# Softmax powers in 16-bit groups of four tiles on VectorE, with TensorE adding two terms

## The chip, the cores and the metric

The kernel runs on one core of one Trainium2 chip. The metric is device time in microseconds (us) for one execution. Before the change three runs took 917.80, 919.02 and 920.45 us; the median is 919.02 us. Engines are named as the profile names them: PE is TensorE (matmul), PEld its weight loads, DVE is VectorE, ACT is ScalarE, POOL is GpSimd, SP issues DMAs.

## The reference

Two attention blocks read the same input `x` (2048 x 512) and are mixed by a gate.

```python
S, D, H, Dh = 2048, 512, 32, 16
g = sigmoid((x * gate_w).sum(-1))                 # one number for each row
# A: linear attention; the feature maps are softmaxes over 16 features, of p and of -p
pq, pk = q @ w_phi, k @ w_phi                     # per head
phi = concat(softmax(p), softmax(-p))             # 32 features, for q and for k
a = (phi_q @ (phi_k.T @ v)) / (phi_q @ sum(phi_k) + 1e-6) @ wo_A
# B: full softmax attention, 32 heads of 16
b = softmax(q @ k.T * 0.25) @ v @ wo_B
out = g * a + (1 - g) * b
```

## The kernel before

Block B carries most of the work. Its scores are computed transposed: a *tile* is 128 keys by 512 queries of one head. The work is cut into 32 *blocks* (4 query chunks x 8 groups of four heads), each of 4 heads x 16 key tiles, so 2048 tiles in all. Four heads lie in four row strips of TensorE, and up to four score products (L624, `qk_mm`, 32 rows each) run side by side in it. The scores are scaled so that the number is already an exponent: multiplied by log2(e) and 2^23.

Tiles are handed out in *slots*. In slot j `add_qk` writes up to three tiles into three PSUM banks of `psS` (banks 0 to 2 for even j, 3 to 5 for odd j), `add_exp` (L687) turns them into powers with one ScalarE instruction over 1536 (or 1024) columns, and `add_pv` (L700) multiplies the powers with the values in four column strips, summing in the bank `psO`. An extra column of ones in `vaug` sums the powers, so that `add_norm` can divide at the block's end. The score product of slot j+2 may start once the exponential of slot j is done.

152 of the 2048 tiles, the *D tiles*, do not go to ScalarE. In a slot with a D tile the exponential covers two tiles and VectorE takes the third bank: `add_d` stores the scaled score as an int32 with the bits of a float (D1, L666), takes the mantissa (D2, L677), and multiplies with a cubic in the mantissa (D4 to D6, L679 to L681). 122 late D tiles go in pairs of 1024 columns in fp32, 30 early ones alone in 512 columns. One value product per D tile is added to a later slot's `add_pv`. The cubic's leading factor is in the exponential's bias.

Block A is cut into small steps that are put between the slots. `phi` makes a feature map for 128 rows: product (L482), VectorE copy to `Pf` (L871), maximum and minimum over 16 features (L875, L877), POOL subtracts twice (L880, L883), ScalarE exponentiates 1024 columns (L886), VectorE sums and inverts (L890, L892), POOL multiplies (L894). It runs 32 times. `q_rest` and `kv_half` do the linear attention, `out_tile`, `out_pre` and `out_post` the output products. All these use one PSUM bank, `psM` (`MISC = [bM]`). The gate is computed in `gate` and multiplied in at the normalisations (`rg` at L765 for B, `nc` at L947 for A).

What sets the order: `Plan.layout` is a list scheduler written in the kernel. It has a guess of each step's duration and a priority, and from these it writes one fixed instruction list per engine, with semaphore waits. On the chip each engine takes its list strictly in that order. Where the plan sees TensorE with too little to do it adds dummy products of 512 columns: in front of a slot's scores (L642) and into `psM` (L1025); 577 in all.

## Time and profile before

| | us |
|---|---|
| median of three runs | 919.02 |
| profiled execution, from first to last instruction | 917.8 |
| ACT busy | 889.2 (97%) |
| PE busy, dummy products among it | 800.0 (87%) |
| DVE busy | 730.3 (80%) |
| POOL busy | 151.2 (16%) |

The span of the profiled execution, 917.8 us, equals the time of the lowest run, so nothing measurable lies around it; it stands 1.2 us under the median. Busy time of an engine counts overlapping instructions once. ACT and DVE instructions overlap a little at their ends, so that the rows by shape add up to more than the engine's busy time.

### The profile page before, as it was taken

Reading aid. Unit: us, or ns where it says so; the run is one execution under the profiler, and the core shown is the slowest. Engines: PE = TensorE matmul, PEld = TensorE weight load, DVE = VectorE, ACT = ScalarE, POOL = GpSimd, SP = SyncE. Lnnn points to the kernel's source line nnn. Section 1 sums busy time; section 2 is a strip of 40 time slices with the busy share of each in tenths; the row PEclk is TensorE's granted clock in tenths of the full one; section 3 lists DMA queues with packets and bytes.
Section 4 is the critical chain, followed back from the end, with each engine's and each line's share of the span. In section 5 each row is a group of like instructions: output and inputs, shape, how many; then the busy total and the mean of one; then the engine's idle time right before and its main releaser. Section 6 shows DMA issues by size and latency. Waiting matters only on the chain.

```text
span 917.8 us, 13911 instructions
## 1 busy us (share of the span) xinstructions
PE 800.0 (87%) x5801; PEld 251.3 (27%) x5903; DVE 730.3 (80%) x1114; ACT 889.2 (97%) x720; POOL 151.2 (16%) x131
## 2 busy tenths in 40 slices
PE   8889889889888889888878978888989998898988
PEld 3232323222222322223223222222222222222222
DVE  2567787788797887978988898799878877787884
ACT  6999999999999999999989999999999999999996
POOL 5000022234155501410330150020000000000000
PEclk9999999999999999999989999999999999999999
DMA  7500000000000000000000000000000000000000
GB/s 138 139 1 1 1 1 2 1 1 1 1 1 1 1 7 6 7 1 7 1 1 1 1 1 1 1 12 7 6 1 2 18 6 1 1 1 1 1 1 23
DMA packets 18959, 9.30 MB, mean 10 GB/s; under 512 B 13265, under 2 KB 18897, under 8 KB 18897
## 3 DMA queue, kind: packets, MB, share of 16 engines
q1 hardware_dynamic: 16928, 8.00, 3.7%
q8 instruction: 46, 0.75, 0.4%
q10 hardware_dynamic: 1584, 0.39, 0.2%
q0 software_dynamic: 384, 0.02, 0.1%
q14 instruction: 17, 0.13, 0.1%
HBM read 3.69 MB, written 2.10 MB: 6 GB/s over the span
## 4 chain that ended last, share of the span: by engine, by line
ACT 72%; DVE 16%; PE 11%; issue 1%
ACT E_t L687 71%; PE psS L624 3%; PE psM L482 3%; DVE stat_t L890 2%; PE psO L700 2%; PE psS L642 1%; DVE vA_t L680 1%; DVE Pf_t L871 1%; DVE vA_t L679 1%; ACT EA_t L886 1%; DVE WB_t L681 1%; DVE vA_t L666 1%; DVE vA_t L677 1%; DVE denr_t L947 1%; DVE stat_t L892 1%
## 5 line engine op out<-in xcount | busy, mean ns | idle before, releaser
L687 ACT ACTIVATE E_t<-psS 128x1536 bf16<-128x1536 f32 (+1 forms) x683 | 861.4, 1406 | 12.4 <-PE psS L624 11.6
L624 PE MATMUL psS<-qz_t,kTB_t 32*128 32x512 bf16 x2048 | 271.0, 387 | 28.0 <-ACT E_t L687 15.3
L700 PE MATMUL psO<-E_t,vaug_t 128*32 128x512 bf16 (+1 forms) x1914 | 268.8, 392 | 0.8 <-ACT E_t L687 0.6
L642 PE MATMUL psS<-WoA_t,ident_t 128*128 128x512 bf16 x327 | 115.6, 390 | 57.0 <-ACT E_t L687 52.3
L666 DVE TENSOR_SCALAR vA_t<-psS 128x512 int32<-128x512 f32 x122 | 83.6, 685 | 56.6 <-PE psS L624 55.7
L624 PEld LDWEIGHTS psS<-qz_t,kTB_t 32*128 32x128 bf16 x2048 | 66.5, 91 | 219.0 <-ACT E_t L687 110.2
L700 PEld LDWEIGHTS psO<-E_t,vaug_t 128*32 128x32 bf16 (+1 forms) x1914 | 65.7, 92 | 154.5 <-issue 141.2
L880 POOL TENSOR_TENSOR Dd_t<-Pf_t,stat_t 128x512 bf16<-128x512 f32 x32 | 37.9, 1186 | 306.5 <-DVE stat_t L875 275.5
L679 DVE SCALAR_TENSOR_TENSOR vA_t<-vA_t 128x1024 f32<-128x1024 f32 x61 | 78.0, 1279 | 1.4
L680 DVE SCALAR_TENSOR_TENSOR vA_t<-vA_t 128x1024 f32<-128x1024 f32 x61 | 76.2, 1248 | 1.0
L681 DVE SCALAR_TENSOR_TENSOR WB_t<-vA_t 128x1024 bf16<-128x1024 f32 x61 | 73.8, 1210 | 0.3
L1025 PE MATMUL psM<-WoA_t,ident_t 128*128 128x512 bf16 x190 | 63.1, 386 | 1.2 <-issue 1.1
L642 PEld LDWEIGHTS psS<-WoA_t,ident_t 128*128 128x128 bf16 x367 | 28.6, 97 | 122.7 <-ACT E_t L687 115.4
L700 PE MATMUL psO<-WB_t,vaug_t 128*32 128x512 bf16 (+1 forms) x122 | 47.2, 392 | 0.0
L894 POOL TENSOR_TENSOR phiQ_t<-EA_t,stat_t 128x1024 bf16<-128x1024 bf16 x16 | 31.5, 1977 | 85.7 <-DVE stat_t L892 67.8
L677 DVE TENSOR_SCALAR vA_t<-vA_t 128x1024 int32<-128x1024 int32 x61 | 44.4, 729 | 1.2
L894 POOL TENSOR_TENSOR phiK_t<-EA_t,stat_t 128x1024 bf16<-128x1024 bf16 x16 | 31.8, 1988 | 64.4 <-DVE stat_t L892 47.8
L482 PE MATMUL psM<-Wp_t,xT_t 128*128 128x512 bf16 x119 | 37.9, 396 | 3.6 <-DVE vA_t L863 1.8
L890 DVE TENSOR_REDUCE stat_t<-EA_t 128x64 f32<-128x1024 bf16 x32 | 38.4, 1205 | 1.5 <-ACT EA_t L886 1.4
L883 POOL TENSOR_TENSOR Dd_t<-stat_t,Pf_t 128x512 bf16<-128x512 f32 x32 | 38.1, 1192 | 0.4 <-DVE stat_t L877 0.4
L482 PE MATMUL psM<-xT_t,WB_t 128*128 128x512 bf16 x109 | 33.2, 384 | 4.3 <-issue 1.0
L760 DVE STREAM_TRANSPOSE Tf_t<-psO 128x512 f32<-128x512 f32 x32 | 22.6, 707 | 17.2 <-PE psO L700 17.1
(109 smaller groups left out, 651.4 us busy)
## 6 DMA issues: line engine op xcount, KB each, us to landing
out_dram<-WvA_t SPq DMA_DIRECT2D x16, 128.0 KB, 1.7
WB_t<-in_B_wqkv_dram SPq DMA_DIRECT2D x3, 384.0 KB, 4.8
Dd_t<-in_A_x_dram SPq DMA_DIRECT2D x4, 128.0 KB, 3.4
WvA_t<-in_A_wqkv_dram SPq DMA_DIRECT2D x1, 512.0 KB, 5.0
WoA_t<-in_A_wo_dram SPq DMA_DIRECT2D x1, 512.0 KB, 5.0
WoB_t<-in_B_wo_dram SPq DMA_DIRECT2D x1, 512.0 KB, 5.9
WB_t<-in_B_wqkv_dram ACTq DMA_DIRECT2D x3, 128.0 KB, 3.4
xT_t<-in_A_x_dram SPq DMA_TRANSPOSE x12, 4.1
```

The lines of the kernel that those rows point to most:

```text
L482: return [lambda e, ap, i=i: e.matmul(ap, lhsT=lhs[i], rhs=rhs[i], start=(i == 0), stop=(i == len(lhs) - 1)) for i in range(len(lhs))]
L624: return e.matmul(bank, lhsT=kT_B[32 * i:32 * i + 32, hg // 2, 128 * kt:128 * (kt + 1)], rhs=qz[32 * i:32 * i + 32, (b // 8) % 2, hg, :], ...
L642: e.matmul(psS[:, 512 * base:512 * (base + 1)], lhsT=ident[:], rhs=WoA[:, 0, :], start=True, stop=True)
L666: add(0.70, -45, lambda e: e.tensor_scalar(dp.t[bt].bitcast(I32)[:, 512 * half:512 * half + 512], bank, EXPB, -2.0 ** 31, op0=ALU.add, op1 ...
L679: add(f2, -20, lambda e: e.scalar_tensor_tensor(u, m, C2, m, op0=ALU.add, op1=ALU.mult), rm, [("U",)], "D4")
L680: add(f2, -20, lambda e: e.scalar_tensor_tensor(u, u, C1, m, op0=ALU.add, op1=ALU.mult), rm + ru, [("U",)], "D5")
L681: add(f2, -20, lambda e: e.scalar_tensor_tensor(dp.e[be][:, 0:w], u, C0, t, op0=ALU.add, op1=ALU.mult), ru + rt, [("E", be)], "D6")
L687: op = P.add("act", 0.07 + 0.000833 * 512 * n, 0.0, lambda e: e.activation(Ebuf[:, j % ERING, 0:512 * n], psS[:, 512 * base:512 * (base + ...
L700: return e.matmul(psO[32 * i:32 * i + w, :], lhsT=vaug[:, kt, VW * h:VW * h + w], rhs=rhs, start=start, stop=stop, tile_position=(0, 32 * ...
L890: P.add("dve", 1.22, prio, lambda e: e.tensor_reduce(stat[:, b, 1, :], e3, AX.X, ALU.add), reads=[("EA", b)], writes=[("ss", b)], name=f"s ...
L894: P.add("pool", 2.0, prio, lambda e: e.tensor_tensor(dst.rearrange("p (g f) -> p g f", f=DH), e3, stat[:, b, 1, :].unsqueeze(2).to_broadca ...
L1025: P.idle = (bM, 0.05, lambda e: e.matmul(psM[:], lhsT=ident[:], rhs=WoA[:, 0, :], start=True, stop=True), P.writer["WoA"][0])
```

## The change

It does six things.

1. The D tiles are *groups*: one key tile for all four heads of a block, 4 x 512 columns. `NG` lists the groups per block, 78 in all, so 312 D tiles; ScalarE keeps 1736 tiles. Blocks 18 to 29 have three and four groups in turn.
2. The arithmetic is 16 bits wide. The score is scaled by 2^7, so that an int16 has the bits of a bf16 number t. Per group VectorE runs D1 four times (512 columns out of PSUM, L671), D2 (mantissa with the exponent of 0.5, L680), D3 (the power of two alone, L682) and D4 (t times D2's result, L684), the last three over 2048 columns. The cubic is gone: the two terms, D3's and D4's, each get a value product, and TensorE sums them in `psO` (`add_pvd`, eight products per group). The bias of the exponential is gone with the cubic's factor.
3. Slots have three and two tiles in turn, with banks 0 to 2 and 3 to 4. The sixth bank, `bS[5]`, joins `psM` as a second bank for everything else. A D tile's scores (`dq`) are products of their own into one of these two banks. The scheduler may let such a product ride: placed directly behind a slot's score products, in a row strip that they leave free; the terms in the same way behind `add_pv`.
4. `phi` has no shift any more: ScalarE exponentiates p and -p straight from PSUM, in two instructions of 512 columns (L877). The copy, the maximum, the minimum and both POOL subtractions go.
5. The gate is one column of small products and one exponential; 1-g multiplies the output rows in `out_tile`, `out_pre` and `out_post`, and e^(logit) multiplies block A in its normalisation. `rg` and `nc` go.
6. The first groups use the buffers of `WoA` and `WoB` and half of `oT` as working space; the two weight loads come after them. Dummy products, 577 before, are 191.

The order on TensorE in the last third of the program, where no step of block A is left. L624 and L700 are the score and value products of a slot, `E_t` holds ScalarE's powers, `WB_t` those of D tiles, L642 is a dummy, L482 an output product. Before:

```order
L624 MATMUL psS<-qz_t,kTB_t 128x512 x3
L700 MATMUL psO<-E_t,vaug_t 32x512 x2
L700 MATMUL psO<-WB_t,vaug_t 32x512
L482 MATMUL psM<-WoB_t,oT_t 128x512 x2
L624 MATMUL psS<-qz_t,kTB_t 128x512 x3
L700 MATMUL psO<-E_t,vaug_t 32x512 x3
L642 MATMUL psS<-WoA_t,ident_t 128x512 x2
```

After, at a like place (L610 and L704 are the same products; `vA_t` and `Tx_t` hold terms of D tiles):

```order
L610 MATMUL psS<-qz_t,kTB_t 128x512 x3
L704 MATMUL psO<-E_t,vaug_t 32x512 x3
L704 MATMUL psO<-vA_t,vaug_t 32x512
L610 MATMUL psS<-qz_t,kTB_t 128x512 x2
L704 MATMUL psO<-E_t,vaug_t 32x512 x2
L704 MATMUL psO<-vA_t,vaug_t 32x512 x3
L704 MATMUL psO<-Tx_t,vaug_t 32x512
L610 MATMUL psS<-qz_t,kTB_t 128x512 x4
L704 MATMUL psO<-E_t,vaug_t 32x512 x3
L704 MATMUL psO<-Tx_t,vaug_t 32x512 x2
L610 MATMUL psS<-qz_t,kTB_t 128x512 x2
L610 MATMUL psM<-qz_t,kTB_t 128x512
```

Slots of three and two tiles now alternate, terms stand directly behind the slot's value products, and a D tile's score product stands behind a slot's (the fourth of "x4", and the one into `psM`).

The order on VectorE in the same part of the program. Before, one pair of late D tiles with the first step of the next:

```order
L666 TENSOR_SCALAR vA_t<-psS 128x512
L677 TENSOR_SCALAR vA_t<-vA_t 128x1024
L679 SCALAR_TENSOR_TENSOR vA_t<-vA_t 128x1024
L680 SCALAR_TENSOR_TENSOR vA_t<-vA_t 128x1024
L666 TENSOR_SCALAR vA_t<-psS 128x512
L681 SCALAR_TENSOR_TENSOR WB_t<-vA_t 128x1024
```

After, one group with steps of its neighbours (L780 belongs to a block's normalisation):

```order
L671 TENSOR_SCALAR Tx_t<-psS 128x512
L780 TENSOR_TENSOR TB_t<-Tf_t,rd_t 128x16x16
L671 TENSOR_SCALAR Tx_t<-psM 128x512
L671 TENSOR_SCALAR Tx_t<-psS 128x512
L680 TENSOR_SCALAR WB_t<-Tx_t 128x2x1024
L682 TENSOR_SCALAR vA_t<-Tx_t 128x2048
L671 TENSOR_SCALAR Tx_t<-psM 128x512
L684 TENSOR_TENSOR Tx_t<-Tx_t,WB_t 128x2048
```

Three fp32 steps with two inputs have become one with 16-bit inputs, and the first steps of D tiles now empty `psM` and `bS[5]` (shown as psS), not a slot's bank.

The diff, cut to what the prediction speaks of:

```diff
-C3 = 0.10644611
-C2 = -6.64634687
-C1 = 12.93904106
-C0 = -16.68089397
-ESCALE = math.log(2.0) / 2.0 ** 23
-EBIAS = -math.log(C3)
-DLAG = 10
-
-D_RATE = ((14, 0.17), (196, 0.0), (226, 0.22), (420, 0.31))
-D_SWITCH = 210
+QSCALE = 0.25 * LOG2E * 2.0 ** 7
+EXPB = 127.0 * 2.0 ** 7 - 75.0
+ESCALE = math.log(2.0) / 2.0 ** 7
+
+NG = (0,) + (2,) * 7 + (1,) + (2,) * 9 + (3, 4) * 6 + (2, 1)
+G_EARLY = 8
+D_FIRST = 12
...
+                ride = None
+                if e == "pe" and last_pe is not None and busy[e] > t - 1e-6:
+                    want = {"qk": "dq", "pv": "term"}[last_pe]
+                    for item in sorted(queues[e]):
+                        o = item[2]
+                        if o.kind == want and not used_heads & set(o.heads):
+                            if o.acq is not None:
+                                bs = [b for b in o.acq.banks if b.free and b.shared]
+                                if not bs:
+                                    continue
+                                o.acq.bank = min(bs, key=lambda b: max([0.0] + [x.end for x in b.last]))
+                            ride = item
+                            break
+                    if ride is not None:
+                        queues[e].remove(ride)
+                        heapq.heapify(queues[e])
+                        pick = ride[2]
+                        pick.dur = RIDE
+                        used_heads |= set(pick.heads)
...
-    MISC = [bM]
+    MISC = [bM, bS[5]]
...
+    groups = [[dict(b=b, kt=NT - 1 - k) for k in range(NG[b])] for b in range(NB)]
...
+        act = [t for t in (next_tile() for _ in range(3 - j % 2)) if t is not None]
...
+    vfree = vAf[:, 0:8192].rearrange("p (n c) -> p n c", c=2048)
+    flat = lambda ap: ap.rearrange("p a b -> p (a b)")
+    bufs = {"x0": (Tx[:, 0, :], ()), "x1": (Tx[:, 1, :], ()), "woA": (flat(WoA[:]), ()), "woB": (flat(WoB[:]), ()),
+            "oT1": (flat(oT[:, 1, :, :]), ()), "a0": (vfree[:, 0, :], va_free), "a1": (vfree[:, 1, :], va_free),
+            "a2": (vfree[:, 2, :], va_free), "a3": (vfree[:, 3, :], va_free),
+            "w0": (W_B[:, 0:2, D:3 * D], kv_mm), "w1": (W_B[:, 2:4, D:3 * D], kv_mm)}
+    rings = {True: (("x0", "x1"), ("woB", "oT1"), "woA"), False: (("x0", "x1", "a0", "a1"), ("w0", "a2", "a3"), "w1")}
+    count = {True: 0, False: 0}
...
-            op.take = [bS[3], bS[4], bS[5]]
+            op.take = [bS[3], bS[4]]
...
+    def add_group(g):
+        b, hg, kt = g["b"], g["b"] % 8, g["kt"]
+        t, s, m = (bufs[g[k]][0] for k in "tsm")
+        ft, ops = opening(g["t"]), []
+        before = list(dq_ops)
+        dq_ops.clear()
+        for q in range(4):
+            f, mm = fill(d_prio(g), [lambda e, ap, q=q: qk_mm(e, (b, q, kt), ap)],
+                         [("kT", hg // 2, kt // 4), ("q", (b // 8) % 2, hg)], name=f"dq{b}.{kt}.{q}", dur=0.27,
+                         after=[exp_ops[D_FIRST]] + ft + P.writer.get((g["t"], q), []) +
+                         P.readers.get((g["t"], q), []) + before, cols=240)
+            dq_ops.append(mm)
+            mm.kind, mm.heads = "dq", [q]
+            ops.append(drain(f, mm, "dve", 0.70, d_prio(g), lambda e, ap, q=q: e.tensor_scalar(
+                quarter(t, q).bitcast(I16), ap, EXPB, 0.0, op0=ALU.add, op1=ALU.max),
+                writes=[(g["t"], q)], after=ft, name=f"D1.{b}.{kt}.{q}"))
+
+        def add(dur, fn, reads, writes, name, after=()):
+            ops.append(P.add("dve", dur, d_prio(g) - 5.0, fn, reads=reads, writes=writes, after=after,
+                             name=f"{name}.{b}.{kt}"))
+        tk = [(g["t"], k) for k in range(4)]
+        mi, si16, ti16 = m.bitcast(I16), s.bitcast(I16), t.bitcast(I16)
+        add(0.72, lambda e: e.tensor_scalar(shaped(mi, mi), shaped(ti16, mi), 0x007F, 0x3F00, op0=ALU.bitwise_and,
+                                            op1=ALU.bitwise_or), tk, [g["m"]], "D2", opening(g["m"]))
+        add(0.72, lambda e: e.tensor_single_scalar(shaped(si16, si16), shaped(ti16, si16), 0x7F80, ALU.bitwise_and),
+            tk, [g["s"]], "D3", opening(g["s"]))
+        add(1.24, lambda e: e.tensor_tensor(shaped(t, m), shaped(t, m), m, ALU.mult), [g["m"]], tk, "D4")
+        if g["early"]:
+            early_ops.extend(ops)
 
     def add_exp(j):
...
-            Ebuf[:, j % ERING, 0:512 * n], psS[:, 512 * base:512 * (base + n)], ACTF.Exp, bias=EBIAS, scale=ESCALE),
+            Ebuf[:, j % ERING, 0:512 * n], psS[:, 512 * base:512 * (base + n)], ACTF.Exp, scale=ESCALE),
...
+    def add_pvd(g, started):
+        b, kt = g["b"], g["kt"]
+        ops = []
+        for which in "st":
+            for i in range(4):
+                ap = quarter(bufs[g[which]][0], i)
+                op = P.add("pe", 0.26, T_PRIO, lambda e, ap=ap, i=i: pv_mm(e, (b, i, kt), ap, False, False),
+                           reads=[(g["t"], i) if which == "t" else g["s"], ("v", (b % 8) // 2, kt // 4), "v1", "v2"],
+                           after=[started], name=f"pvd{which}{i}.{b}.{kt}")
+                op.full = 0.05
+                op.kind, op.heads = "term", [i]
+                ops.append(op)
+        if g["early"]:
+            early_ops.extend(ops)
...
-        P.add("dve", 0.2, -40, lambda e: e.tensor_tensor(rd[:, bb, :], rd[:, bb, :], gT[:, 2, 16 * qc:16 * qc + 16],
-                                                         ALU.mult), reads=[("rd", bb), "omg"], writes=[("rd2", bb)],
-              name=f"rg{b}")
...
-        drain(f, mm, "dve", 0.69, 0, lambda e, ap: e.tensor_copy(fin[:, tile % 4, :], ap),
-              writes=[("fin", tile % 4)], after=va_ops, name=f"Oe{tile}")
+        drain(f, mm, "dve", 0.69, 0, lambda e, ap: e.tensor_scalar(
+            fin[:, tile % 4, :], ap, omg[:, tile:tile + 1], None, op0=ALU.mult),
...
+        drain(f, mm, "act", 0.25, -5, lambda e, ap: e.activation(egate, ap[:, 0:NT], ACTF.Exp), writes=["eg"],
+              name="ge")
+        P.add("dve", 0.1, 20, lambda e: e.tensor_single_scalar(gT[:, 1, :], egate, 1.0, ALU.add), reads=["eg"],
               writes=["g1"], name="g1")
-        P.add("dve", 0.3, 20, lambda e: e.reciprocal(gT[:, 0, :], gT[:, 3, :]), reads=["g1"], writes=["g"], name="g2")
...
-        drain(f, mm, "dve", 0.69, prio, lambda e, ap: e.tensor_copy(Pf[:, b, :], ap), writes=[("Pf", b)],
-              name=f"Pe{qk}.{st}")
-        p3 = Pf[:, b, :].rearrange("p (h f) -> p h f", f=DH)
-        mx, mn = stat[:, b, 0, 0:32], stat[:, b, 0, 32:64]
-        P.add("dve", 0.68, prio, lambda e: e.tensor_reduce(mx, p3, AX.X, ALU.max), reads=[("Pf", b)],
-              writes=[("mx", b)], name=f"mx{qk}.{st}")
-        P.add("dve", 0.68, prio, lambda e: e.tensor_reduce(mn, p3, AX.X, ALU.min), reads=[("Pf", b)],
-              writes=[("mn", b)], name=f"mn{qk}.{st}")
-        dv = Dd[:, b, :].rearrange("p (h f) -> p h f", f=32)
-        P.add("pool", 1.1, prio, lambda e: e.tensor_tensor(
-            dv[:, :, 0:DH], p3, mx.unsqueeze(2).to_broadcast([128, H, DH]), ALU.subtract),
-            reads=[("Pf", b), ("mx", b)], writes=[("D", b, 0)], name=f"d0{qk}.{st}")
-        P.add("pool", 1.1, prio, lambda e: e.tensor_tensor(
-            dv[:, :, DH:32], mn.unsqueeze(2).to_broadcast([128, H, DH]), p3, ALU.subtract),
-            reads=[("Pf", b), ("mn", b)], writes=[("D", b, 1)], name=f"d1{qk}.{st}")
-        ex = P.add("act", 1.2, -4, lambda e: e.activation(EA[:, b, :], Dd[:, b, :], ACTF.Exp),
-                   reads=[("D", b, 0), ("D", b, 1)], writes=[("EA", b)], name=f"ex{qk}.{st}")
-        ex.margin = 1.0
+        def both(e, ap):
+            for sgn in range(2):
+                ins = e.activation(EA[:, b, :].rearrange("p (g s c) -> p s g c", s=2, c=64)[:, sgn, :, :],
+                                   ap.rearrange("p (g c) -> p g c", c=64), ACTF.Exp, scale=1.0 - 2.0 * sgn)
+            return ins
+        drain(f, mm, "act", 0.98, -4, both, writes=[("EA", b)], name=f"ex{qk}.{st}")
...
-            P.add("dve", 0.2, -3, lambda e, dr=dr: e.tensor_tensor(dr, dr, g128[:, i:i + 1].to_broadcast([128, 16]),
-                                                                   ALU.mult),
-                  reads=[("dr", b, rnd), "g128"], writes=[("dr", b, rnd)], name=f"nc{i}.{rnd}")
...
+                return e.scalar_tensor_tensor(dst, num, egate[:, i:i + 1],
+                                              dr3.unsqueeze(3).to_broadcast([128, 4, 4, 16]), ALU.mult, ALU.mult)
```

290 lines of the change are left out of this document (114 added, 176 removed).

## The prediction

> **What bounds the kernel now.** I read the page's busy times and its chain of waits first, then the groups by shape, then ACT's waits, then stretches of time. From the page:
>
> ```profile
> PE 800.0 (87%) x5801; PEld 251.3 (27%) x5903; DVE 730.3 (80%) x1114; ACT 889.2 (97%) x720; POOL 151.2 (16%) x131
> ACT 72%; DVE 16%; PE 11%; issue 1%
> L687 ACT ACTIVATE E_t<-psS 128x1536 bf16<-128x1536 f32 (+1 forms) x683 | 861.4, 1406 | 12.4 <-PE psS L624 11.6
> ```
>
> ScalarE is the bound: 97% busy, and 861.4 of its 889.2 us are the exponentials of L687. They waited 12.4 us in all, nearly all of it for score products. So the change is worth what it takes off ScalarE, less what new waits put into ScalarE's queue. The groups by shape give the prices (count, then busy us and mean ns of one):
>
> ```profile
> L687 ACT ACTIVATE E_t<-psS 128x1536 bf16<-128x1536 f32 x530 | 739.6, 1500 | 10.1 <-PE psS L624 9.3
> L687 ACT ACTIVATE E_t<-psS 128x1024 bf16<-128x1024 f32 x153 | 165.2, 1080 | 2.3 <-PE psS L624 2.3
> L666 DVE TENSOR_SCALAR vA_t<-psS 128x512 int32<-128x512 f32 x122 | 83.6, 685 | 56.6 <-PE psS L624 55.7
> L679 DVE SCALAR_TENSOR_TENSOR vA_t<-vA_t 128x1024 f32<-128x1024 f32 x61 | 78.0, 1279 | 1.4
> L680 DVE SCALAR_TENSOR_TENSOR vA_t<-vA_t 128x1024 f32<-128x1024 f32 x61 | 76.2, 1248 | 1.0
> L681 DVE SCALAR_TENSOR_TENSOR WB_t<-vA_t 128x1024 bf16<-128x1024 f32 x61 | 73.8, 1210 | 0.3
> L677 DVE TENSOR_SCALAR vA_t<-vA_t 128x1024 int32<-128x1024 int32 x61 | 44.4, 729 | 1.2
> L886 ACT ACTIVATE EA_t<-Dd_t 128x1024 bf16<-128x1024 bf16 x32 | 35.8, 1120 | 0.2 <-POOL Dd_t L883 0.2
> L679 DVE SCALAR_TENSOR_TENSOR phiQT_t<-phiQT_t 128x512 f32<-128x512 f32 x30 | 21.1, 703 | 0.5
> L871 DVE COPY Pf_t<-psM 128x512 f32<-128x512 f32 x32 | 21.8, 682 | 10.8 <-PE psM L482 10.6
> L875 DVE TENSOR_REDUCE stat_t<-Pf_t 128x32 f32<-128x512 f32 x32 | 21.5, 671 | 0.5
> L947 DVE TENSOR_TENSOR denr_t<-denr_t,g_t 128x16 f32<-128x16 f32 x32 | 11.3, 354 | 0.6
> L760 DVE STREAM_TRANSPOSE Tf_t<-psO 128x512 f32<-128x512 f32 x32 | 22.6, 707 | 17.2 <-PE psO L700 17.1
> L932 DVE COPY phiQT_t<-psM 128x1024 bf16<-128x1024 bf16 x16 | 11.0, 685 | 6.0 <-PE psM L929 5.7
> ```
>
> Then stretches of time. The columns are the stretch, its length, busy us (and instructions) of PE, PEld, DVE, ACT and POOL, the granted clock, and two of DMA. The last row is clean running late in the program; the others are steps of 3.4 us around places where the clock falls to half, and one where it doesn't:
>
> ```profile
> 367.40:370.80 3.40, 1.59 (x13) 0.51 (x14) 3.40 (x7) 3.39 (x3) 0.00 (x0) 0.99 0.00 0
> 370.80:374.20 3.40, 3.40 (x17) 0.65 (x14) 3.18 (x5) 2.57 (x2) 0.72 (x1) 0.50 0.14 43
> 469.80:473.20 3.40, 1.70 (x12) 0.48 (x12) 3.40 (x6) 3.40 (x3) 1.93 (x1) 0.99 0.02 5
> 473.20:476.60 3.40, 2.63 (x14) 0.68 (x14) 2.20 (x7) 0.81 (x2) 0.00 (x0) 0.50 0.00 0
> 476.60:480.00 3.40, 3.40 (x21) 0.94 (x20) 2.13 (x4) 2.19 (x3) 0.00 (x0) 0.50 0.00 0
> 480.00:483.40 3.40, 3.40 (x25) 1.45 (x25) 2.12 (x3) 3.05 (x3) 1.26 (x1) 0.50 0.00 0
> 230.80:234.20 3.40, 1.96 (x25) 0.88 (x23) 2.65 (x4) 3.40 (x4) 0.00 (x0) 1.00 0.00 0
> 720.00:780.00 60.00, 54.37 (x366) 15.49 (x372) 46.63 (x57) 60.00 (x51) 0.00 (x0) 1.00 0.02 8
> ```
>
> In 720 to 780 us ScalarE never waits. Where it does, a step in which PE was busy for half the time only (1.59, 1.70 us) is followed by steps at clock 0.50, and there ScalarE loses time: 13.6 us from 469.8 to 483.4 held 9.45 us of it, a loss of 4.1 us for 10.2 us at half clock.
>
> **ScalarE, term by term.** The two shapes of L687 differ by one tile of 512 columns and by 1500 - 1080 = 420 ns, so a tile costs 0.420 us. The 683 instructions held 530 x 3 + 153 x 2 = 1896 tiles; 861.4 - 1896 x 0.420 = 65.1 us is left, 0.095 us for an instruction (waits inside the busy time included). After, 312 tiles instead of 152 go to VectorE, so ScalarE has 1736 in 695 instructions:
> - 160 tiles fewer: -67.2 us. 12 instructions more: +1.1 us.
> - Feature maps: 64 instructions of 512 columns for 32 of 1024. The columns are the same; 32 more instructions cost +3.0 us, and reading PSUM (1080 ns for 1024 columns, against 1120 from SBUF) gives back 1.3 us.
> - The bias goes and the gate's exponential is narrower; no row prices either apart, and I take nothing, between -1 and +1 us.
>
> ScalarE's busy time becomes 889.2 - 64.4 = 824.8 us. It was idle for 917.8 - 889.2 = 28.6 us. The start and the end make most of that:
>
> ```profile
> 11.25 9.51 ACT E_t L687 x7
> 904.58 2.70 ACT E_t L687 x2
> 911.21 0.18 DVE rd_t L765
> 912.65 1.04 PE psS L482 x4
> ```
>
> The first exponential starts at 11.25 us, with some 3 us of ScalarE work before it, and the chain after the last (end about 909.5) takes 8.3 us: 8.2 + 8.3 = 16.5 us. The change leaves the first block's loads and projections as they are and takes 0.2 us (L765) from the end: 16.3. Idle in between was 28.6 - 16.5 = 12.1 us, over half of it at half clock. Two things move it.
>
> *Short slots.* Behind a two-tile exponential the next scores have 420 ns less time. ScalarE's whole wait for them was this, beside POOL's and VectorE's on the shared bank:
>
> ```profile
> ACT E_t L687 <- PE psS L624: 11.6, 19, 2.6
> PEld psM L482 <- DVE Pf_t L871: 8.9, 15, 1.6
> ```
>
> 153 short slots become 347. If short slots carried all 11.6 us it would grow by 347/153 to 26 (+15); if they carry none, +0. Late in the program, where nearly one slot in three is short, ScalarE reads 60.00 of 60.00, which is nearer to the lower end: I take +4.
>
> *Clock.* 191 dummies remain of 577, and groups of two tiles fill less of the array. Terms that ride count nothing as time. I take half as much clock loss again, +4; the ends are below.
>
> 824.8 + 16.3 + 12.1 + 8 = **861 us** for the profiled execution; a median would stand about 1 above. Since the per-instruction 0.095 us was taken with waits in it, some of these 8 are counted twice, and I say **858**.
>
> **VectorE: does it hide?** Removed: 456 us of D tiles (83.6 + 78.0 + 76.2 + 73.8 + 44.4 for the late ones; the thirty early ones, five steps of 512 columns at about 0.67 us like L679's 703 ns, 100), 64.8 of L871, L875 and its twin L877, and some 20 of gate factors, L947 the largest. Added: 312 D1 from PSUM at 685 ns, 213.7 us. D2 and D3 are unseen in this form. One input of 1024 int32 took 729 ns where two fp32 inputs took 1279, so single-input work runs at two elements a cycle; and L932 moved 1024 bf16 out of PSUM in 685 ns where L871 moved 512 fp32 in 682, so 16-bit pairs count as one. With both, 2048 columns cost what 1024 int32 did, 0.73 us; with one, 0.73 x 2 less the fixed part (729 - 533 at 0.96 columns per ns), 1.26 us. D4, two 16-bit inputs, is 1.25 us if pairs hold there, or 2.43 us if not (703 ns for 512, 1279 for 1024, on by 1.125 ns each). I take the low ends, since either half has its own row. A group is 2.74 + 0.73 + 0.73 + 1.25 = 5.45 us, 78 of them 425 us, and VectorE's total is 730.3 - 456 - 64.8 - 20 + 425 = 614 us, 72%. The Trainium skill, "VectorE: DVE Perf Modes", section "The perf-mode tier table", gives 693 ns and 1224 ns for 2048 bf16 columns in the two kinds; by that a group is 5.35 us and the time stays the same.
>
> The tight place is blocks 18 to 29, with 42 groups: 229 us and some 45 us of other VectorE work (12 transposes like L760 at 0.71 us and about 90 smaller steps), against 600 tiles in 240 instructions on ScalarE, 600 x 0.420 + 240 x 0.095 = 275 us. VectorE is at the same length by durations; its instructions overlap at their ends, which brings it some way under. It fits, with nothing to spare; the cover for D1 to D4 there is ScalarE's 275 us. Who waits if it slips: a D tile's score product needs a bank that D1 has emptied, and behind it in PE's list stand the slot's value products and the next scores.
>
> **TensorE.**
>
> ```profile
> 800.79 0.39 PE L624 MATMUL psS<-qz_t,kTB_t 32*128 32x512 bf16 x3
> 801.12 0.40 PE L700 MATMUL psO<-E_t,vaug_t 128*17 128x512 bf16 x3
> 801.45 0.39 PE L1025 MATMUL psM<-WoA_t,ident_t 128*128 128x512 bf16 x1
> 907.96 0.39 PE L700 MATMUL psO<-E_t,vaug_t 128*32 128x512 bf16 x3
> 907.97 0.39 PE L700 MATMUL psO<-WB_t,vaug_t 128*32 128x512 bf16 x1
> 909.20 0.60 PE L1025 MATMUL psM<-WoA_t,ident_t 128*128 128x512 bf16 x2
> ```
>
> Three score products side by side take 0.33 us from start to start, as do three value products; a fourth in a free strip starts 0.01 us behind (907.97); a product that must queue adds 0.21 us (0.60 against 0.39). In the new order 300 of 312 D score products and 488 of 624 terms stand where a strip is free; the other 148 add 31 us, 24 more groups of slots 8. PE's real work rises by some 40 us on about 620 (800.0 less 577 dummies at 0.31). 660 of 858 us is 77%: no bound at full clock. SP and POOL: the two weight loads move behind the early groups, ready before the first output product; POOL loses 64 subtractions and nothing waits for what is left.
>
> **Rivals.**
> - *VectorE without the doubled rates of D2 and D3.* Then +1.06 us for each of 42 late groups, all beyond the cover: 858 + 42 = 900. For it: no row shows 16-bit data at four elements a cycle. If D4 also ran at 2.43 us, another 42 x 1.18 = 50 less what overlaps, 930 to 945.
> - *PE held by D1.* 312 new waits on two banks. The fifteen waits above cost 0.6 us each; one in five of 312 at 0.6 us, half of it covered: +19, 877. Against: two banks in place of one.
> - *The clock drops in blocks 18 to 29 (the other side).* A step with PE busy under some 1.7 of 3.4 us came before each fall; 1.96 us (230.8) did not suffice. The late stage loses most of its dummies. At half clock a score or value group takes 0.21 us more than its 0.33, so PE's work there, some 15 us of 23 per block, becomes 25, and with its waits 27 to 30: were all twelve blocks at half, +50 to +85 us, 908 to 943, mostly slower than before. At 0.40 us lost for each us at half clock (4.1 of 10.2) it decides at (918 - 854) / 0.40 = 160 us of half clock, 47 steps; five are there now. A moderate case, 20 steps, gives 854 + 27 = 881. The Trainium skill, "TensorE: Matmul & The Clock Gate", section "Why this matters for your kernels", allows idle gaps up to about 3 us before the clock falls; by that no step would fall here and the time would be 851, but the rows at 367.4 and 469.8, with half the step busy, were enough.
> - *The short slots cost nothing and the clock holds*: 861 - 8 - 7 = 846.
>
> **How the numbers follow.** The forecast with its own range, 842 to 870: 0.62. D2 and D3 slow: 0.08. PE held by D1: 0.12. Moderate clock loss: 0.11. Slower than before, by the clock (0.04) or by D2 to D4 together (0.02): 0.06. Equal within 0.3%, about what this measurement can tell from no change: 0.01. The range 842 to 890 leaves out the slow D2 and D3, the slower cases and a little below. Faster 0.93, same 0.01, slower 0.06.
>
> **What would show it.** ACT busy near 825 us, with 347 exponentials of 1536 columns and 347 of 1024; D2 and D3 near 0.73 us and D4 near 1.25; VectorE between 600 and 640 us busy; clock at 1.00 but for a few steps; ACT's wait for scores under 25 us. Wrong if D2 takes 1.26 us, if the clock stands at 0.5 for tens of steps, or if the scores' waits behind D1 pass 30 us.

## The result, and the profile after

After the change four runs have a median of 849.62 us (842.10 to 855.81), beside 919.34 us for the kernel before on the same chip: a ratio of 0.9219, 95% interval 0.9177 to 0.9261. Ten runs of the changed kernel, from two series, are used below. The profiled execution has a span of 848.7 us and a time of 850.53; each run's time stands about 1.8 us above its own span. Each ratio in this document is worked out from the single runs and leaves out those more than 1.5% above the fastest of their kernel (here the one of 855.81 us), so it is not the quotient of the two medians.

From the page of after: busy times, the engines on the chain that ended last, and the exponentials of the slots (L691, which were L687).

```profile
PE 757.7 (89%) x5877; PEld 230.0 (27%) x5877; DVE 608.7 (72%) x973; ACT 823.5 (97%) x764; POOL 75.1 (9%) x60
ACT 82%; PE 14%; DVE 4%; issue 0%; ACTq 0%
L691 ACT ACTIVATE E_t<-psS 128x1536 bf16<-128x1536 f32 (+1 forms) x695 | 795.8, 1306 | 8.5 <-PE psS L610 8.0
```

ScalarE is still the bound and still 97% busy; it only has less to do, 823.5 us instead of 889.2. The span fell by 69.1 us, ScalarE's busy time by 65.7. The groups by shape of after (busy us, mean ns of one):

```profile
L691 ACT ACTIVATE E_t<-psS 128x1536 bf16<-128x1536 f32 x347 | 526.7, 1518 | 7.4 <-PE psS L610 7.0
L691 ACT ACTIVATE E_t<-psS 128x1024 bf16<-128x1024 f32 x347 | 380.2, 1096 | 1.2 <-PE psS L610 1.0
L671 DVE TENSOR_SCALAR Tx_t<-psM 128x512 int16<-128x512 f32 x91 | 62.2, 683 | 30.9 <-PE psM L610 29.2 <-PE psS L610 1.4
L680 DVE TENSOR_SCALAR WB_t<-Tx_t 128x2048 int16<-128x2048 int16 x32 | 23.3, 728 | 0.5
L680 DVE TENSOR_SCALAR WB_t<-vA_t 128x2048 int16<-128x2048 int16 x32 | 21.9, 686 | 0.5
L682 DVE TENSOR_SCALAR vA_t<-vA_t 128x2048 int16<-128x2048 int16 x21 | 14.3, 682 | 0.2 <-PE psO L704 0.2
L684 DVE TENSOR_TENSOR Tx_t<-Tx_t,WB_t 128x2048 bf16<-128x2048 bf16 x32 | 42.2, 1320 | 0.0
L684 DVE TENSOR_TENSOR vA_t<-vA_t,WB_t 128x2048 bf16<-128x2048 bf16 x32 | 38.8, 1211 | 0.1
```

A tile is still (1518 - 1096) = 0.422 us of ScalarE, and the four steps of a group have the forecast durations: D1 0.68, D2 0.69 to 0.73, D3 0.68 (0.79 in eleven of its 78), D4 1.21 to 1.32 us.

The waits of after, first ScalarE's for scores, then TensorE's for a bank that D1 has to empty:

```profile
ACT E_t L691 <- PE psS L610: 8.0, 18, 1.2
PEld psS L610 <- DVE Tx_t L671: 4.4, 14, 1.0
PEld psS L610 <- DVE vA_t L671: 2.5, 8, 0.8
PEld psM L610 <- DVE Tx_t L671: 2.2, 8, 0.5
```

Then stretches of time in after, with the columns as in the prediction. The first seven lie around the places where the clock fell: at clock 1.00 the 3.4 us step ahead of each of the four falls, at 0.50 steps behind two of them. The last two are stretches of 60 us of clean running:

```profile
56.50:59.90 3.40, 2.73 (x60) 1.71 (x57) 1.35 (x3) 3.40 (x4) 0.00 (x0) 1.00 0.00 0
59.90:63.30 3.40, 2.94 (x36) 1.05 (x32) 3.29 (x6) 3.40 (x5) 0.00 (x0) 0.50 0.02 5
551.40:554.80 3.40, 2.19 (x18) 0.67 (x15) 3.10 (x5) 3.40 (x4) 0.00 (x0) 1.00 0.00 0
660.60:664.00 3.40, 2.36 (x23) 0.68 (x17) 3.37 (x6) 3.40 (x4) 0.00 (x0) 1.00 0.00 0
664.00:667.40 3.40, 3.40 (x19) 0.55 (x15) 1.95 (x3) 2.88 (x3) 0.00 (x0) 0.50 0.00 0
667.40:670.80 3.40, 3.40 (x20) 0.65 (x17) 0.68 (x2) 2.48 (x2) 0.00 (x0) 0.50 0.00 0
722.10:725.50 3.40, 2.24 (x14) 0.60 (x14) 3.38 (x7) 3.40 (x4) 0.00 (x0) 1.00 0.00 0
600.00:660.00 60.00, 52.58 (x429) 15.05 (x428) 51.37 (x82) 60.00 (x55) 1.98 (x1) 1.00 0.03 10
780.00:840.00 60.00, 55.32 (x374) 15.18 (x374) 21.72 (x33) 60.00 (x55) 0.00 (x0) 1.00 0.01 3
```

At full clock ScalarE runs without a gap (60.00 of 60.00) even from 600 to 660 us, in the blocks with three and four groups, where VectorE is busy for 51.37. In the two steps at half clock from 664.0 us TensorE is busy throughout and ScalarE for 2.88 and 2.48 us of 3.40; in the one from 59.9 us ScalarE loses nothing.

One step of before belongs beside these. The clock fell to half at 206.9 us, directly behind it:

```profile
203.50:206.90 3.40, 2.01 (x15) 0.60 (x15) 3.35 (x5) 3.40 (x4) 2.05 (x3) 1.00 0.00 0
```

### The profile page after: what moved, and what is told of

The parts are those of the page before. It is cut to its first block, busy times and chain, and to the rows that moved or that the text cites. A ratio compares the mean times of both kernels' runs of the same rounds, so it can differ in the third digit from the quotient of the medians.

```text
span 848.7 us, 13702 instructions
## 1 busy us (share of the span) xinstructions
PE 757.7 (89%) x5877; PEld 230.0 (27%) x5877; DVE 608.7 (72%) x973; ACT 823.5 (97%) x764; POOL 75.1 (9%) x60
## 4 chain that ended last, share of the span: by engine, by line
ACT 82%; PE 14%; DVE 4%; issue 0%; ACTq 0%
ACT E_t L691 79%; PE psS L610 4%; PE psO L704 3%; ACT EA_t L877 2%; PE psS L498 2%; PE psM L498 1%; PE psS L627 1%; PE psM L418 1%; DVE stat_t L882 1%; DVE Tx_t L684 1%; DVE Tx_t L671 0%; PE psM L1018 0%; PE psM L610 0%; DVE WB_t L680 0%; DVE oA_t L943 0%
## 5 line engine op out<-in xcount | busy, mean ns | idle before, releaser
L691 ACT ACTIVATE E_t<-psS 128x1536 bf16<-128x1536 f32 (+1 forms) x695 | 795.8, 1306 | 8.5 <-PE psS L610 8.0
L610 PE MATMUL psS<-qz_t,kTB_t 32*128 32x512 bf16 x1897 | 285.2, 391 | 47.6 <-ACT E_t L691 40.0
L704 PE MATMUL psO<-E_t,vaug_t 128*32 128x512 bf16 x1736 | 264.0, 396 | 0.0
L610 PEld LDWEIGHTS psS<-qz_t,kTB_t 32*128 32x128 bf16 x1897 | 69.9, 91 | 275.1 <-ACT E_t L691 216.0
L704 PEld LDWEIGHTS psO<-E_t,vaug_t 128*32 128x32 bf16 (+1 forms) x1736 | 61.3, 93 | 144.9 <-issue 138.5
L627 PE MATMUL psS<-xT_t,ident_t 128*128 128x512 bf16 x153 | 60.2, 404 | 32.2 <-ACT E_t L691 30.8
L671 DVE TENSOR_SCALAR Tx_t<-psS 128x512 int16<-128x512 f32 x93 | 63.3, 681 | 30.8 <-PE psS L610 24.4
L671 DVE TENSOR_SCALAR Tx_t<-psM 128x512 int16<-128x512 f32 x91 | 62.2, 683 | 30.9 <-PE psM L610 29.2
L704 PE MATMUL psO<-vA_t,vaug_t 128*32 128x512 bf16 (+1 forms) x296 | 70.5, 396 | 0.0
L610 PE MATMUL psM<-qz_t,kTB_t 32*128 32x512 bf16 x151 | 59.2, 392 | 0.5 <-DVE Tx_t L671 0.2
L671 DVE TENSOR_SCALAR vA_t<-psS 128x512 int16<-128x512 f32 x68 | 46.4, 682 | 13.5 <-PE psS L610 11.5
L671 DVE TENSOR_SCALAR vA_t<-psM 128x512 int16<-128x512 f32 x60 | 40.9, 682 | 17.2 <-PE psS L610 9.5
L704 PE MATMUL psO<-Tx_t,vaug_t 128*32 128x512 bf16 (+1 forms) x184 | 48.3, 384 | 0.0
L684 DVE TENSOR_TENSOR Tx_t<-Tx_t,WB_t 128x2048 bf16<-128x2048 bf16 x32 | 42.2, 1320 | 0.0
L684 DVE TENSOR_TENSOR vA_t<-vA_t,WB_t 128x2048 bf16<-128x2048 bf16 x32 | 38.8, 1211 | 0.1
L498 PE MATMUL psS<-Wp_t,xT_t 128*128 128x512 bf16 x80 | 24.8, 384 | 0.0
L680 DVE TENSOR_SCALAR WB_t<-Tx_t 128x2048 int16<-128x2048 int16 x32 | 23.3, 728 | 0.5
```

What stands on the lines that cost most here:

```text
L498: return [lambda e, ap, i=i: e.matmul(ap, lhsT=lhs[i], rhs=rhs[i], start=(i == 0), stop=(i == len(lhs) - 1)) for i in range(len(lhs))]
L610: return e.matmul(bank, lhsT=kT_B[32 * i:32 * i + 32, hg // 2, 128 * kt:128 * (kt + 1)], rhs=qz[32 * i:32 * i + 32, (b // 8) % 2, hg, :], ...
L627: e.matmul(psS[:, 512 * base:512 * (base + 1)], lhsT=ident[:], rhs=xT[:, 0, 0:NQ], start=True, stop=True)
L671: ops.append(drain(f, mm, "dve", 0.70, d_prio(g), lambda e, ap, q=q: e.tensor_scalar(quarter(t, q).bitcast(I16), ap, EXPB, 0.0, op0=ALU.ad ...
L680: add(0.72, lambda e: e.tensor_scalar(shaped(mi, mi), shaped(ti16, mi), 0x007F, 0x3F00, op0=ALU.bitwise_and, op1=ALU.bitwise_or), tk, [g[" ...
L684: add(1.24, lambda e: e.tensor_tensor(shaped(t, m), shaped(t, m), m, ALU.mult), [g["m"]], tk, "D4")
```

## The experiments

All ratios are to the kernel before, measured on the same chip; "after" is the changed kernel of the section above. The order of the instructions is fixed before the run, and nearly every edit here makes the scheduler lay it out anew; that turned out to matter.

**Half the groups.** 38 groups are 152 D tiles, as many as before the change, with everything else of it kept.

```diff
-NG = (0,) + (2,) * 7 + (1,) + (2,) * 9 + (3, 4) * 6 + (2, 1)
+NG = (0,) + (1,) * 17 + (2, 1) * 6 + (2, 1)
```

> The changed kernel with 38 groups for 78, so 152 D tiles as before the change; all else (16-bit steps, two banks, alternating slots, shiftless feature maps, gate) stays. Theory A (the time is ScalarE's work: 0.420 us a tile, 0.095 us an instruction): 160 tiles and 64 exponentials more than the changed kernel, ScalarE busy 823.5 + 67.2 + 6.1 = 897 us, time about 849 + 73 = 922 us, no faster than before the change. Rival B (the gain comes from VectorE, POOL and the shared bank being relieved): these stay relieved, even more so, and the time stays under 890 us.

918.84 us, ratio 0.9999 (0.9974 to 1.0023). Page of this kernel:

```profile
PE 840.8 (92%) x5944; PEld 259.8 (28%) x5944; DVE 422.7 (46%) x693; ACT 893.8 (98%) x828; POOL 73.5 (8%) x60
```

The whole gain is gone although VectorE has 308 us less to do than before the change. The 160 tiles that left ScalarE carry the 70 us; all other parts together are worth nothing that can be measured when ScalarE's tiles stay. ScalarE's 893.8 is 4.6 above the 889.2 of before: 76 more exponentials (759 for 683) at the prediction's 0.095 us are 7.2. Its idle time is smaller, 20.0 us (913.8 - 893.8) for 28.6.

**The feature maps alone.** The kernel before, with `phi`'s two exponentials taken straight from PSUM and its copy, maximum, minimum and subtractions removed.

```diff
-        drain(f, mm, "dve", 0.69, prio, lambda e, ap: e.tensor_copy(Pf[:, b, :], ap), writes=[("Pf", b)],
...
-        ex = P.add("act", 1.2, -4, lambda e: e.activation(EA[:, b, :], Dd[:, b, :], ACTF.Exp),
...
+        drain(f, mm, "act", 0.98, -4, both, writes=[("EA", b)], name=f"ex{qk}.{st}")
```

> The kernel before the change with one part of it alone: the feature maps exponentiated from PSUM by ScalarE without shift (no copy, maximum, minimum, no POOL subtraction). Theory A: ScalarE's busy time moves by +1.7 us only, VectorE's falls by 65 us and nobody waited for it: 919 us, within 0.5% of before. Rival B: VectorE's 65 us and POOL's 76 us were in the way of block A's steps on the one bank: 10 to 30 us faster, 890 to 909 us.

912.98 us, ratio 0.9929 (0.9908 to 0.9951): 6.5 us, more than the first theory allowed and less than the second. Page and ScalarE's wait for scores:

```profile
PE 821.9 (90%) x5909; PEld 250.7 (27%) x5909; DVE 665.0 (73%) x1018; ACT 890.2 (98%) x752; POOL 80.0 (9%) x67
ACT E_t L687 <- PE psS L624: 5.1, 14, 0.6
```

65 us off VectorE and 71 off POOL leave ScalarE as busy as before (890.2); it waits 6.5 us less for scores (5.1 for 11.6), with the granted clock at 0.996 in the mean. A part of the gain goes with the clock: runs of the kernel before at 0.996 have spans of 913.5 to 915.3 us, this one 912.1. In the half-group kernel such a gain and the 76 additional exponentials would about cancel.

**D2 twice.** Each group does its second step a second time with the same result, 0.7 us more of VectorE for each of 78 groups.

```diff
+        add(0.72, lambda e: e.tensor_scalar(shaped(mi, mi), shaped(ti16, mi), 0x007F, 0x3F00, op0=ALU.bitwise_and,
+                                            op1=ALU.bitwise_or), tk, [g["m"]], "D2b")
```

> The changed kernel with D2 done a second time in every group: 78 more VectorE steps of 2048 columns, 0.70 us each, 55 us in all, 28 us of them in blocks 18 to 29. Theory A as predicted (the late stage has nothing to spare, VectorE's length there equal to ScalarE's): +20 to +30 us, about 870 to 878 us. Rival (VectorE has slack there too, some 10% by its busy time of 51 to 53 us in 60): +0 to +8 us, 849 to 857 us.

872.53 us, ratio 0.9494 (0.9470 to 0.9518), 23 us over after and in the range of the first theory, which laid it to the length of VectorE's work in the whole late stage. The trace shows single places. ScalarE's waits for value products, a stretch of 60 us and a piece of TensorE's list from it (start us, us, what it did, and in brackets what it waited for; L693 and L706 are L691 and L704 here, moved by two lines):

```profile
ACT E_t L693 <- PE psO L706: 19.8, 7, 7.6
620.00:680.00 60.00, 49.93 (x352) 13.62 (x352) 46.56 (x76) 46.64 (x41) 0.00 (x0) 0.91 0.02 8
665.32 0.62 PE L706 MATMUL psO<-WB_t,vaug_t 128*32 128x512 bf16 x4 [0.81 <-DVE WB_t L682]
666.53 0.60 PE L610 MATMUL psS<-qz_t,kTB_t 32*128 32x512 bf16 x1 [0.59 <-DVE Tx_t L671]
668.26 0.60 PE L610 MATMUL psM<-qz_t,kTB_t 32*128 32x512 bf16 x1 [1.13 <-DVE Tx_t L671]
669.88 1.45 ACT L693 ACTIVATE E_t<-psS 128x1536 bf16<-128x1536 f32 x1 [7.60 <-PE psO L706]
```

13.4 us of ScalarE's idle time (46.8 in all, 25.2 in after) lie in this one stretch, in which VectorE is busy for 46.56 of 60 us only. There TensorE's list holds score products of two groups, one behind the other, each waiting for D1, which stands in turn between the D2, D3 and D4 of the group ahead. The slots' value products wait behind them, the powers' buffers stay full, and ScalarE stands for 7.6 us. In these 7.6 us VectorE itself works almost without a gap, so there its length does count. Whether a VectorE that is busy for 43 us longer (651.3 for 608.7) would cost something in a better order, this run does not tell.

**One bank instead of two.** Slots of three tiles throughout, and everything else in `psM` again, D tiles' scores among it.

```diff
-    MISC = [bM, bS[5]]
+    MISC = [bM]
...
-        act = [t for t in (next_tile() for _ in range(3 - j % 2)) if t is not None]
+        act = [t for t in (next_tile() for _ in range(3)) if t is not None]
...
```

> The changed kernel with slots of three tiles throughout, six banks for them, and one bank instead of two for everything else; 78 groups as they are. 579 exponentials for 695, so ScalarE has 11 us less to do. Theory A (two banks carry the D tiles' extra traffic, and PE held by D1 is what the second bank avoids): every D score product waits until D1 has emptied the one bank, PE's list stands, 20 us or more slower, 870 us or more. Rival (the second bank is not needed and the short slots only cost): 838 us.

1071.91 us, ratio 1.1667 (1.1635 to 1.1698). ScalarE has 4.3 us less to do than in after (819.2 us, 579 exponentials), and it waits for products:

```profile
ACT E_t L691 <- PE psO L704: 128.8, 22, 25.7
ACT EA_t L877 <- PE psM L498: 90.9, 10, 26.6
DVE Tx_t L671 <- PE psM L610: 116.1, 124, 3.3
```

With one bank each D1 (0.68 us) and the product that fills the bank take turns, and all else on TensorE stands behind: its weight loads for score products into `psM` wait 89.8 us for D1 (47.6 + 42.2), where after has 3.2. So 312 D tiles need the second bank, bought with the short slots. Slots of three tiles also leave fewer strips free for riding; how much of the loss that is, this run does not tell.

**No dummies.**

```diff
-        self.idle, self.rate, self.inslot = None, 0.57, 0.12
+        self.idle, self.rate, self.inslot = None, 0.0, 0.12
```

> The changed kernel without the 191 dummy products (the order around them is planned anew). Theory A (the clock falls after a step with PE busy for about half the time, and ScalarE loses 0.2 to 0.4 us for each us at half clock): several times the 34 us of half clock of the changed kernel, 100 to 250 us, mean clock 0.85 to 0.94, and 20 to 60 us slower, 870 to 910 us. Rival (the rule that only an idle step drops the clock): clock as it is, dummies only cost PE time, 843 to 850 us.

870.66 us, ratio 0.9468 (0.9417 to 0.9519): 21 us over after, at the low end of the first theory.

```profile
PE 761.9 (88%) x5686; PEld 219.6 (25%) x5686; DVE 603.3 (70%) x973; ACT 825.9 (96%) x764; POOL 76.4 (9%) x60
ACT E_t L691 <- PE psS L610: 17.8, 33, 1.5
```

TensorE does 191 products less and is busy for longer, since the granted clock averages 0.904 (after: 0.98). So the 191 dummies, with the order that comes with them, are worth 21 us. In the profiled executions there are 132 us more at half clock (166 for 34, each 2 x (1 - clock) x span), and the span is 14.4 us longer: 0.11 us for one.

**More dummies.** The same constant at 0.66: 297 dummies.

> The changed kernel with 297 dummy products for 191. Theory A: half clock falls from 34 us to under 10, and at 0.31 us lost per us at half clock (854.0 us at clock 0.970 and 840.2 at 0.996 in the timed runs of the changed kernel) the median falls by 5 to 9 us, to 841 to 845, with less spread from run to run. Rival (the spread has another cause, and 106 more products of 0.21 us crowd the short slots): 850 to 860 us.

864.10 us, ratio 0.9397 (0.9339 to 0.9454): a miss of both theories, 14 us slower than after. The clock stayed as it was (0.982). What came is mostly one wait:

```profile
ACT E_t L691 <- PE psO L704: 8.7, 1, 8.7
785.50 1.03 PE L498 MATMUL psM<-WoB_t,oT_t 128*128 128x512 bf16 x4
786.89 2.36 ACT L691 ACTIVATE E_t<-psS 128x1024 bf16<-128x1024 f32 x2 [8.73 <-PE psO L704]
```

The second row is the last of eight output products (L498, four matmuls each) that stand one behind the other in the new order from 779.46 us on, with a slot's value products behind them. ScalarE had no free buffer for powers until those were done.

**More groups, by hand.** 84 groups, with three in blocks 3, 4 and 9 to 12.

```diff
-NG = (0,) + (2,) * 7 + (1,) + (2,) * 9 + (3, 4) * 6 + (2, 1)
+NG = (0,) + (2,) * 2 + (3,) * 2 + (2,) * 3 + (1,) + (3,) * 4 + (2,) * 5 + (3, 4) * 6 + (2, 1)
```

> The changed kernel with 84 groups for 78 (blocks 3, 4 and 9 to 12 get three instead of two), where VectorE was busy 37 to 43 us in 60. Theory A: 24 tiles and 10 instructions less on ScalarE, -11.0 us: busy 812.5 us, 838 us if VectorE hides them. Rival (VectorE or PE becomes the bound around blocks 9 to 12, where the feature maps crowd): 845 to 860 us.

878.86 us, ratio 0.9561 (0.9502 to 0.9620), a miss of both theories. ScalarE's busy time is the forecast one (812.8), 10.7 us less than after, but its idle time is 32 us more (870.2 - 812.8 = 57.4 for 25.2). ScalarE's two worst waits, the stretch of the longest, and pieces of TensorE's list in it:

```profile
ACT E_t L691 <- PE psO L704: 15.5, 9, 5.6
ACT EA_t L877 <- PE psS L498: 13.5, 1, 13.5
300.60:314.10 13.50, 8.94 (x37) 2.10 (x38) 13.03 (x22) 0.86 (x1) 0.00 (x0) 0.63 0.00 1
303.98 0.60 PE L610 MATMUL psM<-qz_t,kTB_t 32*128 32x512 bf16 x1 [0.21 <-DVE vA_t L671]
306.38 0.60 PE L610 MATMUL psM<-qz_t,kTB_t 32*128 32x512 bf16 x1 [1.20 <-DVE vA_t L671]
308.11 0.60 PE L610 MATMUL psS<-qz_t,kTB_t 32*128 32x512 bf16 x1 [0.58 <-DVE vA_t L671]
311.30 0.60 PE L610 MATMUL psM<-qz_t,kTB_t 32*128 32x512 bf16 x1 [1.20 <-DVE Tx_t L671]
313.03 1.46 PE L498 MATMUL psS<-Wp_t,xT_t 128*128 128x512 bf16 x3 [0.59 <-DVE Tx_t L671]
```

Here three groups stand in TensorE's list without a slot's scores between them. For 13.5 us TensorE goes at VectorE's pace (13.03 us busy), the product for a feature map comes last (L498), and ScalarE, whose next instruction is that map's exponential, does nothing. It is the prediction's rival "PE held by D1", in one place. Where the nine waits for value products (15.5 us) come from is not shown.

**More groups, placed.** If such places carry the loss, more groups must pay where the list has none. Three kernels, in which each block's count was chosen so that no stretch of TensorE's list between two slots' scores is longer than 2.4 us by the rows' durations; beside them the changed kernel again. Each `NG` line with + is one kernel, with its count of groups behind it; the one with 85 has a slightly lower constant for dummies as well.

```diff
-NG = (0,) + (2,) * 7 + (1,) + (2,) * 9 + (3, 4) * 6 + (2, 1)
+NG = (0, 2, 2, 2, 2, 2, 2, 2, 1, 2, 2, 3, 2, 2, 3, 2, 2, 2, 3, 4, 3, 4, 3, 4, 3, 4, 3, 4, 3, 4, 2, 1)   # 80
+NG = (0, 2, 2, 2, 2, 2, 2, 2, 1, 2, 2, 2, 2, 2, 2, 2, 3, 2, 3, 4, 3, 4, 3, 4, 3, 4, 3, 4, 3, 4, 3, 3)   # 82
+NG = (0, 2, 2, 2, 2, 2, 2, 2, 1, 2, 2, 2, 2, 2, 3, 2, 3, 3, 3, 4, 3, 4, 3, 4, 3, 4, 3, 4, 3, 4, 3, 4)   # 85
-        self.idle, self.rate, self.inslot = None, 0.57, 0.12
+        self.idle, self.rate, self.inslot = None, 0.55, 0.12                                             # 85 only
```

> The changed kernel once more, as the measure for the three kernels beside it. All theories: between 842 and 856 us, as in its four runs, with the clock's falls deciding where.

> 80 groups (two more), placed so that no stretch of TensorE's list between two slots' scores is longer than 2.4 us by the durations of the rows; the changed kernel's longest is 2.3, that of 84 groups 5.7. Theory A (ScalarE's tiles carry the time, and the loss with 84 groups came from single pile-ups in TensorE's list): 8 tiles and 3 exponentials fewer, -3.7 us, 843 to 849, ACT busy 820, no wait of ScalarE above 3 us. Rival B (groups beyond 78 cost by themselves, since VectorE can't hide them; 29 us for six groups with 84): 10 us for two groups less 3.7, 855 to 860.

> 82 groups, placed in the same way. Theory A: 16 tiles and 7 exponentials fewer, -7.4 us, 839 to 846, ACT busy 816. Rival B: four groups at 5 us less 7.4, 860 to 865, with waits of ScalarE for scores or products of 20 us and more.

> 85 groups, one more than the kernel with 84 that took 879 us, placed so that no stretch is longer than 2.4 us. Theory A: 28 tiles and 12 exponentials fewer, -12.9 us, 833 to 842, ACT busy 811; four groups in the last block may add up to 5 us at the end. Rival B: 30 us of waits as with 84, 865 to 880.

| | us, median of six | ratio to before (95%) | ACT busy | clock in the profile |
|---|---|---|---|---|
| 78, as changed | 847.06 | 0.9224 (0.9193 to 0.9255) | 823.5 | 0.980 |
| 80 | 841.26 | 0.9171 (0.9145 to 0.9197) | 817.9 | 0.994 |
| 82 | 848.51 | 0.9240 (0.9212 to 0.9268) | 815.6 | 0.984 |
| 85 | 841.73 | 0.9145 (0.9112 to 0.9177) | 809.0 | 0.988 |

Rows of the waits of 80 groups, of 82 and a stretch of 82, then the page of 85 and its wait for scores:

```profile
ACT E_t L691 <- PE psS L610: 1.7, 4, 0.5
```

```profile
ACT E_t L691 <- PE psS L610: 7.7, 13, 2.2
ACT E_t L691 <- PE psO L704: 4.6, 3, 2.2
480.00:540.00 60.00, 50.59 (x392) 15.88 (x394) 47.82 (x82) 55.38 (x53) 7.84 (x4) 0.89 0.00 1
```

```profile
PE 712.0 (85%) x5790; PEld 222.0 (27%) x5865; DVE 635.5 (76%) x1022; ACT 809.0 (97%) x752; POOL 74.6 (9%) x60
ACT E_t L691 <- PE psS L610: 3.2, 8, 0.5
```

85 groups have one more than the kernel of 879 us and take 842, with 3.2 us of waits for scores. So groups past 78 do not cost by themselves; the loss with 84 came with the order of its list. The rival's 855 us and more are out for 80 and 85: 85 lies at the upper end of the first theory's range, 80 even 1.7 us below it. A part of 80's gain is the clock's: at the clock of 0.994 that its profile had, a run of the changed kernel has a span of 841.6, and 80 groups have 838.9, 2.7 us less. For 85 groups the runs at 0.976 have 840.4, and the changed kernel at 0.98 has 848.8. 82 misses the forecast by 2.5 us: its ScalarE work fell by 7.9 us, its idle time rose by 5.1 (845.9 - 815.6 = 30.3 for 25.2), and 4.6 of that idle time lie in the one stretch with the clock at 0.89. That a list without long stretches loses nothing is therefore not a rule. By its interval the kernel with 85 groups is faster than the changed kernel (0.9177 at the most, the changed kernel 0.9193 at the least); between 85 and 80 the intervals overlap, and the medians differ by 0.5 us.

**Without riding.** The scheduler no longer puts a D tile's score product or term directly behind a slot's products in a free strip.

```diff
-                    want = {"qk": "dq", "pv": "term"}[last_pe]
+                    want = "none"
```

> The changed kernel without riding: D tiles' score products and terms stand in TensorE's list by themselves, in the order of their priorities, and no longer directly behind a slot's products in a strip that is free. Theory A (riding is what makes 312 more score products and 624 terms fit beside ScalarE): 788 products no longer lie beside others; if a quarter of them still find a neighbour by chance the rest cost 0.11 to 0.21 us each, 65 to 125 us of TensorE's time, against some 90 us that TensorE has free, and its list has longer pieces between two slots' scores: ScalarE waits 25 to 70 us for scores and products, 872 to 915 us, with ACT busy at 823. Rival B (TensorE is not the bound, its free time and its dummies take it up): 843 to 858, with fewer dummies.

1083.94 us, ratio 1.1801 (1.1753 to 1.1849): the direction of the first theory at more than three times its highest price (234 us over after, where it had up to 65). Page, granted clock in 40 slices, and ScalarE's waits:

```profile
PE 946.5 (88%) x5914; PEld 257.6 (24%) x5914; DVE 610.1 (56%) x973; ACT 836.4 (77%) x764; POOL 73.5 (7%) x60
PEclk9988999878799899977899895685977759777599
ACT E_t L691 <- PE psO L704: 151.0, 32, 16.2
ACT E_t L691 <- PE psS L610: 38.6, 67, 1.5
```

TensorE is busy for 189 us more with about as many products (5914 for 5877); the granted clock averages 0.837, which is some 350 us at half clock. Counted in the two traces, 1842 score and value products start more than 0.03 us behind the one ahead of them, for 1587 in after. That is 255 more, so most of the 788 products of the expectation still found a neighbour. Longer pieces of the list and the clock come together here, and the run does not tell how much each took.

## Why the prediction was right, and where not

It said 858 us, between 842 and 870 for the likeliest case; 849.6 came, by the mechanism that it named: ScalarE stays the bound, and its tiles carry the gain. Its sum against the profiled execution:

| term | forecast us | measured us |
|---|---|---|
| ACT busy | 824.8 | 823.5 |
| idle at start and end | 16.3 | 17.0 (8.5 + 8.5) |
| idle in between | 12.1 + 8 | 8.2 (848.7 - 823.5 - 17.0) |
| sum | 861.2 | 848.7 |

- *ScalarE's tiles.* Right: 347 exponentials of each shape, 823.5 us, and the half-group kernel shows that these tiles carry the whole gain. The two feature-map instructions and the bias were rightly small.
- *The short slots, +4.* Wrong. The slots of two tiles are 347 instead of 153, and ScalarE waits 8.0 us for scores instead of 11.6; the half-group kernel has 379 of them, and 3.2 us of these waits at a clock of 0.993. The waits stand where the prediction put them, ahead of the long exponentials, which follow a short one (7.0 us, against 1.0 ahead of the short ones), but they did not grow with their number. What the first step put at nothing, fewer steps on VectorE and POOL for the feature maps, is worth 6.5 us in the kernel before, as much as these waits fell there, a part of it by the clock.
- *The clock, +4.* Mis-sized twice. It did fall for longer, 34.1 us in ten steps instead of 17.1 in five, where half as much again was allowed. But a microsecond of it cost less than the 0.40 of the rows before: from 664.0 to 681.1 ScalarE lost 3.7 us of 17.1. Over the ten runs of the changed kernel, whose half-clock time is 2 x (1 - clock) x span, the span goes from 840.2 at 7 us to 854.0 at 51 us, 0.31 us for one. So 7 us of half clock go with 840 and 34 with 849, and the runs' spread follows the clock. The price holds for one order only: without dummies it was 0.11. 840.2 is 823.5 + 16.7, the start and the end: with the clock up hardly anything is left in between.
- *The mark for the falls* was wrong. The prediction had "PE busy under some 1.7 of 3.4 us" before each fall in before. Two of the three steps there have 1.59 and 1.70, but the one at 203.5 us, shown with the result, has 2.01, more than the 1.96 that was followed by none. After, the four steps ahead of a fall have 2.73, 2.19, 2.36 and 2.24. No idle gap of 3 us, on which the Trainium skill ("TensorE: Matmul & The Clock Gate", "Why this matters for your kernels") lets the clock fall, fits into such a step, so that rule does not tell these falls. The same page of the Trainium skill, section "A second HAM failure mode: psum-queue depth-cycling", tells of a kernel whose clock fell and rose through short idle times between its matmuls; these rows are of that kind, with 0.7 to 1.2 us idle in a step of 3.4. The Trainium skill's section "What's actually happening" on that page has a window of 3.4 us that runs free of the kernel; the steps here have that length, but that the window's place makes one run fall where another does not, no run shows. What share of a step decides stays open.
- *VectorE.* 608.7 us against 614, and D2 and D3 at doubled rates: the rival that had them at 1.26 us is out (its 900 us had a slip: 42 x 1.06 is 44.5, so 902). "The perf-mode tier table" of "VectorE: DVE Perf Modes" in the Trainium skill gives 693 and 1224 ns; the rows have 679 to 728 (790 for eleven of D3) and 1211 to 1320. "It fits, with nothing to spare" was too narrow: VectorE is busy for 51.37 of 60 us from 600 to 660 and 52.89 in the densest stretch, 720 to 780, and 85 groups (635.5 us) fitted as well.
- *PE held by D1.* In the changed kernel the three rows above hold 9.1 us of TensorE's waits, hardly any of it ScalarE's. The rival is real all the same: it took 13.5 us in one place with 84 groups and 7.6 with D2 twice. The prediction priced it as many small waits; it comes as a few long ones, where score products of two or three groups stand in a row.
- *TensorE, "no bound at full clock"*, held, and riding is needed for it: without it, and at the lower clock that came along, the kernel is 18% slower than before. Less its dummies TensorE is busy for 686 us (757.7 - 60.2 - 11.3) where 660 were forecast. The 31 us put on the products that do not ride cannot be read apart in the trace.
- *The time around the span* was put at nothing; it is 1.8 us, in the kernel before as well: a run of 919.66 us there has a span of 917.8.
